# A lightweight convolution with a gated feed-forward on one core: the last values of the first pair put ahead of a multiply, and a new order of work for all later pairs

## The chip, the core and the metric

The kernel runs on one core of a Trainium2 chip. The core has TensorE (PE in the profile; its weight loads are listed apart as PEld), VectorE (DVE), ScalarE (ACT), GpSimd (POOL) and SyncE (SP), which issues most DMAs. The metric is the device time of a run in microseconds, the median of several runs. Lower is better.

## The reference

The input x has 8 sequences of 4096 tokens with 192 features, in float32. First comes a causal convolution over 7 tokens, whose taps are shared by each of 8 groups of 24 features (the kernel takes softmax of the taps once), then an RMS norm and a gated feed-forward:

```
w = softmax(weight, axis=-1)                      # 8 heads x 7 taps
y[b,s,h,g] = sum_k w[h,k] * x[b, s-6+k, h, g]     # zeros ahead of the sequence
xn  = y / sqrt(mean(y*y) + 1e-6) * rms_g          # over the 192 features
g   = xn @ w_gate                                 # 192 x 1536
val = xn @ w_val                                  # 192 x 1536
out = (silu(g) * val) @ w_out                     # 1536 x 192
```

The matrices arrive as 8-byte floats and are converted to 4-byte floats by the kernel itself (convert, L279): a few bit operations on VectorE, three activations on ScalarE, and for w_out an addition (L310) and a multiplication (L311) on GpSimd.

## The kernel before, in words

The 32768 tokens are worked on as 32 pairs, each of two blocks of 512 tokens (g = 0 and 1). Partitions 0 to 63 and 64 to 127 of TensorE's rows work at the same time on two halves: half 0 computes gates, half 1 values. Each half has four of the eight PSUM banks; `pick` and `free` decide which bank is handed out, in the order of the program.

**The first pair (pair 0)** is computed in the plain way by `plain` (L1001 products, L1011 silus on ScalarE, L1018 values = product times silu on VectorE), while the weights are still being converted. The string START says in which order parts are issued: p a product, s a silu, v a value, w a sum of weights, i/o/O conversions, c the convolution of pair 1, n one of five parts of the norm of pair 1 (square, reduce, factor, spread, scale; the last, `scale`, is the multiply of the outputs y by their factors, L499 on GpSimd), and t the placing of the normed pair 1 in DRAM (`place`, L623: eight DMAs, four of them for this pair alone on ScalarE's queue). LATER is a list of such letters with a due time each; it is merged with the output products of pair 0 (`outer`, L1034), with the taps of the convolution of pair 2 (`part_tap`, L429: the first tap on ScalarE, L437, six on VectorE, L445, summed up in a PSUM bank, the last one written to y), with its norm and with eleven sums of X (`x_sum`, L670), all by due time. `outer` has 12 row blocks per product, four products per output group; its values leave the banks by L1049 (ScalarE) and L1053 (VectorE).

**Pairs 1 to 31** use a scheme with fewer products. The class `Pair` runs 4 `Unit`s, which share chains of matrix products (`CHAINS`, L718): a product (v, i) adds the product of weight sum WAT[i] and X sum XOP[i] into bank v of the unit. Between the products the content of a bank is copied. Letters of the actions, each with the unit and half behind it (S42.1.0 is snapshot 42, half 1, unit 0):

- S: a snapshot of a bank into a tile; F: a fork, a copy of a bank into a new bank from which another chain goes on (`FORK`, with a sign)
- D: adds snapshot 00 to bank 5; C: bank 5 plus snapshot 40
- R: bank v plus or minus a snapshot (`RESULT`), a final gate (half 0) or value (half 1), which gives the bank free
- G: silu of a gate; M: value times gate
- S1 to S4 with one number: sums of h for the output (`Pair.sum`, L917); X: sums of X; cv: a tap (`part_tap`) of the pair after next; C1, s7, c2, C21, C22, T11 to T22: steps of the output; Dst0, Dst1: stores; DfetA, DfetB, Dplace, Dload: other DMAs; sq, red, pow, bc, mul: the five parts of the norm

A pair has 120 products (60 chain places x 2 halves, L757) and then nine output forms (`OUTS`, L889). The whole order is written out by hand in the string ORDER: p2 means two products of TensorE, A, V, G and D ahead of a name mean ScalarE, VectorE, GpSimd and a DMA; a name with a minus belongs to the pair before. Each engine works through its own instructions in that order.

Lines that the change and the prediction touch: ORDER, CHAINS, `Unit.do` (L763 to L804: S and F at L708/L712, D L773, C L777, R L781, G L794, M L801), START, LATER and the list `xat` of the X sums at the end.

Of the kernel before, what the change touches and what calls it, by code (L numbers as in the profile page):

```python
# [13 lines left out]
ALU = mybir.AluOpType  # L14
# [5 lines left out]
def kernel(  # L20
# [10 lines left out]
    nc = tc.nc  # L31
# [56 lines left out]

    SPAN = 1509
    ORDER = (  # L90
        "p2 VT11- p2 AS40.1.0 AS40.0.0 p2 Vbc- AF0.0.0 GX9- AF0.1.0 Dst0- p2 VC.1.0 Dload- GX4- VC.0.0 p2",
        "AS41.0.0 VS41.1.0 p1 AS00.0.0 p1 Gmul- VT21- AS00.1.0 p2 VD5.0.0 AS42.0.0",
        "VS42.1.0 p2 VD5.1.0 AS51.0.0 p2 Dst1- VR1.0.0 AS51.1.0 p2 VR1.1.0 AF2.0.0",
        "p2 AF2.1.0 VR0.0.0 Dplace- AG1.0.0 p1 VR0.1.0 p1 AF3.0.0 AF3.1.0 p2 VR2.0.0 AG0.0.0",
        "p1 VR2.1.0 p1 AS44.0.0 GM0.1.0 AS44.1.0 p2 VR3.0.0 AG2.0.0 GM1.1.0 p1 VR3.1.0 p1",
        "AS40.0.1 VR5.0.0 AS40.1.1 p2 AG4.0.0 VR5.1.0 AG5.0.0 p1 VM4.1.0 p1 AF0.0.1 VF0.1.1",
        "p2 AS41.0.1 VM5.1.0 AS41.1.1 p2 GM2.1.0 VC.0.1 AG3.0.0 p1 VC.1.1 p1 AS00.0.1 GM3.1.0",
        "AS00.1.1 p2 AS42.0.1 VS42.1.1 p2 GS3.0 VD5.0.1 p1 VD5.1.1 AS51.0.1 p1 GS3.1 VR1.0.1",
        "AS51.1.1 p2 VR1.1.1 AF2.0.1 p1 GS1.0 p1 AF2.1.1 VR0.0.1 AG1.0.1 p1 VR0.1.1 p1",
        "AF3.0.1 GM1.1.1 AF3.1.1 p2 VR2.0.1 p1 VR2.1.1 GS2.0 p1 AS44.0.1 AS44.1.1 p2 VR3.0.1",  # L100
        "AG0.0.1 p1 VR3.1.1 GM0.1.1 p1 AS40.0.2 VR5.0.1 AS40.1.2 p2 AG4.0.1 VR5.1.1 AG2.0.1",
        "p1 VM4.1.1 p1 AF0.1.2 GM2.1.1 VF0.0.2 p2 AS41.0.2 VS41.1.2 AG3.0.1 p2 VC.0.2 AG5.0.1",
        "GM3.1.1 p1 VC.1.2 p1 AS00.1.2 VS00.0.2 p1 GM5.1.1 p1 AS42.0.2 AS42.1.2 p2 VD5.0.2",
        "GS3.2 p1 VD5.1.2 AS51.0.2 p1 VR1.0.2 AS51.1.2 GS1.1 p2 VR1.1.2 AF2.0.2 p2 AF2.1.2",
        "VR0.0.2 GS1.2 AG1.0.2 p1 VR0.1.2 p1 AF3.0.2 GS2.1 AF3.1.2 p2 VR2.0.2 AG0.0.2 p1",
        "VR2.1.2 p1 AS44.0.2 GM0.1.2 AS44.1.2 p2 VR3.0.2 GM1.1.2 p1 VR5.1.2 p1 AS40.0.3",
        "VR5.0.2 AS40.1.3 p2 GS2.2 AG4.0.2 VR3.1.2 AG3.0.2 p1 VM4.1.2 p1 AG5.0.2 VF0.0.3 p2",
        "AF0.1.3 GM5.1.2 VS41.1.3 AS41.0.3 p2 AG2.0.2 VC.0.3 p1 VC.1.3 p1 AS00.0.3 VM2.1.2",
        "AS00.1.3 p2 AS42.0.3 GM3.1.2 AS42.1.3 p2 VD5.0.3 GS3.3 p1 VD5.1.3 AS51.0.3 p1",
        "VR1.0.3 AS51.1.3 p2 GS4.2 VR1.1.3 AF2.0.3 p2 AF2.1.3 VR0.0.3 GS1.3 p1 VR0.1.3 p1",  # L110
        "AF3.0.3 VF3.1.3 p2 GS3.4 AS44.1.3 VS44.0.3 AG1.0.3 p2 VR5.1.3 AG0.0.3 GM1.1.3 p1",
        "VR5.0.3 p1 VR3.0.3 AG5.0.3 p1 GS2.3 VR3.1.3 AG4.0.3 p2 Acv0_2 VM4.1.3 p2 Acv0_0",
        "GS4.3 VR2.0.3 DfetA p1 Acv0_1 p1 Vcv1_0 p1 AG3.0.3 p1 GM5.1.3 Vcv1_2 p3 VM3.1.3 p1",
        "Ac1 p1 GS3.5 Vcv2_0 p2 Vcv2_2 p2 GS1.4 Vcv1_1 p3 VM0.1.3 p2 GS1.5 Vcv2_1 p2 As7",
        "Vcv3_0 DfetB p1 AG2.0.3 p1 Vcv3_1 GS2.5 p2 Vcv3_2 p2 GS2.4 Vcv4_0 p2 VR2.1.3 p2",
        "GS4.0 Vcv4_2 p2 Vcv5_0 p2 GS4.4 p4 VX0 Ac2 p2 GS4.1 Vcv5_2 p2 Vcv4_1 p1 GX1 p1",
        "Vcv5_1 p2 Vcv6_0 p1 GM2.1.3 p1 Vcv6_2 p3 GX7 p3 GX3 p2 VC22 p2 Vcv6_1 p2 VT22 Asq p2",
        "VX2 p2 GS4.5 VC21 p1 Vred p2 GX6 p5 VX5 p2 VX8 p2 VX10 p1 Gpow VT12 p2",
    )

    cst = ctx.enter_context(tc.tile_pool(name="cst", bufs=1))
# [115 lines left out]
    def load_out(i):  # L237
# [28 lines left out]
        out=taps[:], in0=w_sb[:], in1=stat[:].to_broadcast([P, H, K]), op=ALU.subtract  # L266
# [7 lines left out]
        out=taps[:], in0=taps[:], in1=ssum[:].to_broadcast([P, H, K]), op=ALU.mult  # L274
# [419 lines left out]
    def put(at, do):  # L694
        heapq.heappush(line, (at, next(tick), do))
# [5 lines left out]
    def plus(s):  # L701
        return ALU.add if s > 0 else ALU.subtract
# [3 lines left out]
    def copy(eng, dst, src, s=1):  # L706
        if eng == "A":
            nc.scalar.activation(out=dst, in_=src, func=AF.Copy, scale=float(s))  # L708
        elif s < 0:
            nc.vector.tensor_scalar(out=dst, in0=src, scalar1=-1.0, scalar2=None, op0=ALU.mult)  # L710
        else:
            nc.vector.tensor_copy(out=dst, in_=src)  # L712
# [5 lines left out]
    CHAINS = [  # L718
        [(u, 4, 11)] + [(u - 1, 4, 0)] * (u > 0) + [(u, *c) for c in CHAIN] for u in range(NU)
    ]  # L720
    CHAINS[0][2:4] = CHAINS[0][3:1:-1]
    CHAINS[0][5:7] = CHAINS[0][6:4:-1]
    CHAINS[-1][-3:] = [(NU - 1, 4, 12), (NU - 1, 2, 1), (NU - 1, 3, 14), (NU - 1, 4, 0)]
    FORK = {0: (1, 1), 2: (4, 1), 3: (5, -1)}
    RESULT = {1: ("42", -1), 0: ("41", -1), 2: ("51", -1), 5: ("44", -1), 3: ("c", 1)}

    class Unit:
        def __init__(self, u):
            self.u = u
            self.ht = None  # L730
            self.bk, self.tl = {}, {}

        def new(self, v, h, product=False):
# [29 lines left out]
        def do(self, eng, act, h):  # L763
            tl, kind, v = self.tl, act[0], int(act[1:2] or 0)
            if kind == "S":
                t = tl[act[1:], h] = tiles.pop(0)
                copy(eng, t[:], self.old(v, h))
            elif kind == "F":
                src, s = FORK[v]
                copy(eng, self.new(v, h), self.old(src, h), s)  # L770
            elif kind == "D":
                b, t = self.old(5, h), tl.pop(("00", h))
                nc.vector.tensor_tensor(out=b, in0=b, in1=t[:], op=ALU.add)  # L773
                tiles.append(t)
            elif kind == "C":
                t = tl["c", h] = tl.pop(("40", h))
                nc.vector.tensor_tensor(out=t[:], in0=self.old(5, h), in1=t[:], op=ALU.add)  # L777
            elif kind == "R":
                k, s = RESULT[v]
                t = tl.pop((k, h))  # L780
                nc.vector.tensor_tensor(  # L781
                    out=self.hv(v) if h else t[:], in0=self.old(v, h), in1=t[:], op=plus(s)
                )
                self.leave(v, h)
                if h:
                    tiles.append(t)
                else:
                    tl["g", v] = t
            elif kind == "G":
                if v in RESULT:  # L790
                    t = src = tl["g", v]
                else:
                    t, src = tiles.pop(0), self.old(v, 0)
                nc.scalar.activation(out=t[:], in_=src[:], func=AF.Silu)  # L794
                if v not in RESULT:
                    self.leave(v, 0)
                tl["g", v] = t
            else:
                t = tl.pop(("g", v))
                src = self.hv(v) if v in RESULT else self.old(v, 1)  # L800
                engine[eng].tensor_tensor(out=self.hv(v), in0=src, in1=t[:], op=ALU.mult)  # L801
                if v not in RESULT:
                    self.leave(v, 1)
                tiles.append(t)  # L804
# [311 lines left out]
    def done(it):  # L1116
# [8 lines left out]

    START = (
        "XxxxxxXDdDdDTDdadTbTaTfbTakTakTakTkbkKkKkKkbkbfpoffpfsicpsvivOpsipisvicpsvpvwsicwpvs"
        "iwpvscwpsiwvpisvicpsvovpwispvswcipvwspsiwOvpsiwvipsvvpswopsvcpsvOnovoOpsonvOpsnoOvnopsoOn"
    )
    LATER = (  # L1130
        (55, "O"), (60, "t"), (163, "s"), (170, "O"), (200, "v"), (294, "v"),
        (463, "w"), (564, "w"), (664, "w"), (764, "w"), (864, "w"), (964, "w"), (1064, "w"),
        (1164, "w"), (1264, "w"),
    )
# [9 lines left out]
    p, sl, v = plain(hts)  # L1144
# [37 lines left out]
    for j in range(len(SIDE)):  # L1182
        put(c + 240 + 700 * (j // 2), functools.partial(part_tap, 2, 0, j))
        for k in range(1, K):
            at = c + 250 + 100 * k + 50 * j if j < 2 else c + 960 + 80 * k
# [3 lines left out]
    later(place(2), c + 2450)  # L1189
    xat = [c + i for i in (1660, 1730, 2060, 2130, 2200, 2270, 2290)]  # L1190
    xat += [c + i for i in (2360, 2370, 2380, 2390)]
    for i, at in enumerate(xat):
        put(at, functools.partial(x_sum, i))
    later(out_sums(), *[base + 2600 + 60 * i for i in range(4 * NM)])
    emit(float("inf"))
# [48 lines left out]
```

## Time and profile before

| | |
|---|---|
| median of 3 runs | 2607.96 us (2606.99 to 2608.02) |
| profiled execution, own time | 2610.66 us |
| its span | 2608.7 us |
| TensorE busy | 2575.5 us (99%), 23794 instructions |
| VectorE busy | 2272.6 us (87%), 3617 |
| ScalarE busy | 1618.6 us (62%), 2967 |
| GpSimd busy | 2081.1 us (80%), 1693 |
| TensorE clock granted, mean | 0.997 |

The span runs from the first to the last event of one profiled execution on the core; the execution's own time is 2 us longer than it, and 2.7 us longer than the median of the runs. Busy time says how long an engine had an instruction in work; where an engine is not the one that the others wait for, its idle time costs nothing. The granted clock is the share of full speed that the throttle of TensorE allowed. A time in the timeline counts from the start of the span.

### The profile page before, as it was taken

The numbers are of one execution on the slowest core, as the hardware profiler recorded it, in microseconds if no ns is written. First come the engines' busy times: TensorE is split into PE (matmuls) and PEld (weight loads), VectorE is DVE, ScalarE is ACT, GpSimd is POOL, SyncE is SP. The second block draws the span as 40 slices with busy tenths as digits, with TensorE's granted clock in tenths as the row PEclk, the third lists the DMA queues.
The fourth block names the chain that finished last, engine by engine and source line by source line (L and its number), as shares of the span: only waits on it lengthen the run. The fifth ranks groups of instructions, "written<-read, shape, count | busy, mean of one in ns | idle before, by whom it ended". The sixth has DMA issues, their size and how long they took to land.

```text
span 2608.7 us, 60700 instructions
## 1 busy us (share of the span) xinstructions
PE 2575.5 (99%) x23794; PEld 1869.1 (72%) x23794; DVE 2272.6 (87%) x3617; ACT 1618.6 (62%) x2967; POOL 2081.1 (80%) x1693
## 2 busy tenths in 40 slices
PE   6999999999999999999999999999999999999999
PEld 3677777777777766777777777777777777777776
DVE  8988888988888988898888889888888888888875
ACT  5375556765556765557655567655577555676554
POOL 3878788877888777888788887778887888887776
PEclk9999999999999999999999999999999999999999
DMA  6313321323312223213233122232132332232210
GB/s 144 56 39 57 63 47 42 63 39 63 63 35 54 51 51 63 50 39 63 39 63 63 37 52 51 51 63 52 38 61 40 62 63 42 47 60 41 50 38 13
DMA packets 512603, 137.36 MB, mean 53 GB/s; under 512 B 484284, under 2 KB 486844, under 8 KB 512189
## 3 DMA queue, kind: packets, MB, share of 16 engines
q1 hardware_dynamic: 509068, 132.80, 26.7%
q8 instruction: 186, 3.05, 0.5%
q10 hardware_dynamic: 3248, 0.69, 0.1%
q14 instruction: 101, 0.83, 0.1%
HBM read 83.87 MB, written 49.55 MB: 51 GB/s over the span
## 4 chain that ended last, share of the span: by engine, by line
PE 97%; DVE 2%; DMA 0%; ACT 0%; issue 0%; DVEq 0%; SPq 0%; ACTq 0%
PE ps L757 62%; PE ps L889 33%; PE ps L1041 1%; PE ps L1001 1%; DVE xc L304 0%; DMA x<-in_x_dram 0%; DVE ht L1018 0%; DVE y L406 0%; DVE y L421 0%; DVE y L394 0%; PE ps L595 0%; DVE wf L319 0%; ACT xb L615 0%; DVE xc L314 0%; DVE xc L287 0%
## 5 line engine op out<-in xcount | busy, mean ns | idle before, releaser
L757 PE MATMUL ps<-xc,wf 64*128 64x512 f32 x4960 | 1250.0, 592 | 0.0
L757 PEld LDWEIGHTS ps<-xc,wf 64*128 64x128 f32 x4960 | 755.4, 186 | 308.8 <-issue 66.2
L757 PE MATMUL ps<-xb,wf 64*128 64x512 f32 x2480 | 710.4, 589 | 0.0
L801 POOL TENSOR_TENSOR ht<-ht,tile 128x512 f32<-128x512 f32 x298 | 378.8, 1280 | 277.1 <-ACT tile L794 275.1
L708 ACT ACTIVATE tile<-ps 128x512 f32<-128x512 f32 (+1 forms) x677 | 391.0, 593 | 319.5 <-PE ps L757 190.1
L708 ACT ACTIVATE tls<-ps 128x512 f32<-128x512 f32 (+1 forms) x656 | 376.1, 589 | 314.9 <-PE ps L889 192.7
L757 PEld LDWEIGHTS ps<-xb,wf 64*128 64x128 f32 x2480 | 391.9, 187 | 143.6 <-issue 30.7
L708 ACT ACTIVATE ps<-ps 128x512 f32<-128x512 f32 (+1 forms) x651 | 366.9, 578 | 54.0 <-PE ps L889 39.0
L917 POOL TENSOR_TENSOR early<-ht 128x512 f32<-128x512 f32 x279 | 379.4, 1365 | 4.9
L889 PE MATMUL ps<-ht,wo_sb 128*32 128x128 f32 (+2 forms) x5208 | 318.6, 380 | 0.0
L445 DVE SCALAR_TENSOR_TENSOR ps<-xh,tp,ps 128x512 f32<-128x512 f32 x450 | 312.0, 745 | 1.2
L801 POOL TENSOR_TENSOR ht<-ht,tls 128x512 f32<-128x512 f32 x198 | 251.6, 1277 | 76.2 <-ACT tls L794 74.6
L781 DVE TENSOR_TENSOR tile<-ps,tile 128x512 f32<-128x512 f32 x366 | 250.1, 687 | 62.8 <-PE ps L757 56.1
L889 PEld LDWEIGHTS ps<-ht,wo_sb 128*32 128x32 f32 x5208 | 234.2, 110 | 81.5 <-POOL ht L801 23.5
L889 PE MATMUL ps<-ht,x 128*32 128x128 f32 (+2 forms) x4464 | 250.7, 379 | 0.0
L917 POOL TENSOR_TENSOR ht<-ht 128x512 f32<-128x512 f32 x186 | 248.2, 1351 | 0.0
L794 ACT ACTIVATE tile<-tile 128x512 f32<-128x512 f32 x366 | 228.2, 629 | 12.5 <-DVE tile L781 12.5
L889 PEld LDWEIGHTS ps<-ht,x 128*32 128x32 f32 x4464 | 184.6, 110 | 61.1
L781 DVE TENSOR_TENSOR ht<-ps,tile 128x512 f32<-128x512 f32 x322 | 219.1, 681 | 0.1
L781 DVE TENSOR_TENSOR ht<-ps,tls 128x512 f32<-128x512 f32 x298 | 202.7, 680 | 0.0
L889 PE MATMUL ps<-early,x 128*32 128x256 f32 (+2 forms) x3348 | 196.0, 379 | 0.0
L781 DVE TENSOR_TENSOR tls<-ps,tls 128x512 f32<-128x512 f32 x254 | 173.9, 685 | 25.1 <-PE ps L757 23.6
(129 smaller groups left out, 3176.9 us busy)
## 6 DMA issues: line engine op xcount, KB each, us to landing
xb<-xd SPq DMA_DIRECT2D x124, 384.0 KB
xd<-yn SPq DMA_DIRECT2D x244, 96.0 KB
xh<-in_x_dram SPq DMA_DIRECT2D x192, 105.0 KB
out_dram<-o_sb SPq DMA_DIRECT2D x122, 96.0 KB
out_dram<-o_sb SPq DMA_DIRECT2D x62, 128.0 KB
xh<-in_x_dram SPq DMA_DIRECT2D x56, 98.4 KB
out_dram<-o_sb SPq DMA_DIRECT2D x122, 32.0 KB
ht<-in_moe_w_gate_dram SPq DMA_DIRECT2D x12, 192.0 KB
```

Source lines behind the costliest of these rows:

```text
L445: nc.vector.scalar_tensor_tensor(out=dst, in0=xk, scalar=w, in1=at, op0=ALU.mult, op1=ALU.add)
L708: nc.scalar.activation(out=dst, in_=src, func=AF.Copy, scale=float(s))
L757: nc.tensor.matmul(out=self.new(v, h, True) if first else self.old(v, h), lhsT=wf[self.u][HALF[h], WAT[i], :], rhs=x_op(XOP[i])[HALF[h]], ...
L781: nc.vector.tensor_tensor(out=self.hv(v) if h else t[:], in0=self.old(v, h), in1=t[:], op=plus(s))
L794: nc.scalar.activation(out=t[:], in_=src[:], func=AF.Silu)
L801: engine[eng].tensor_tensor(out=self.hv(v), in0=src, in1=t[:], op=ALU.mult)
L889: nc.tensor.matmul(out=self.bank(b)[i * Q : (i + 1) * Q, at : at + n], lhsT=left, rhs=cols, start=fresh, stop=True, skip_group_check=True, ...
L917: engine[eng].tensor_tensor(out=dst, in0=a, in1=b, op=op)
L1001: nc.tensor.matmul(out=bank(h, bks[h])[:], lhsT=wf[u][HALF[h], k * NF + f, :], rhs=xb[HALF[h], g, k, :], start=(k == 0), stop=(k == KP - 1 ...
L1041: nc.tensor.matmul(out=bank(h, bks[h])[:, w : w + D], lhsT=hts[f // NF][HALF[h], g, f % NF, j * P : (j + 1) * P], rhs=wo_sb[HALF[h], f, :] ...
```

## The change

The change has four parts.

1. In unit 0 of every pair the products (4,7) and (0,3) change places, so that (4,7) stands directly ahead of (5,2) and (2,1).
2. The upper half of bank 2 in unit 0 is no longer a copy of bank 4 (AF2.1.0 is gone). A new action N on VectorE takes snapshot 51 of the upper half away from bank 4; product (2,1) then finds no bank for (2, upper half), takes one with start=True and so begins afresh; and R2 adds the snapshot instead of subtracting it. The value is the same. Units 1 to 3 keep the fork.
3. ORDER is new. Per pair ScalarE has 87 actions instead of 92, VectorE 108 instead of 106, GpSimd 51 instead of 48. Snapshots S00.0.0, S00.0.1, S41.0.1, S41.0.3, S42.0.3, S44.1.3 and forks F3.0.1, F3.0.2, F3.0.3 go to VectorE; S00.0.2, S41.1.3, S44.0.3, F0.0.3 and F3.1.3 go to ScalarE; the multiplies M0.1.3, M2.1.2, M3.1.3 and M5.1.0 go to GpSimd, M2.1.3 to VectorE; X0, X2 and X8 go to GpSimd, X1, X3 and X6 to VectorE. The place DMAs, the stores, the norm's parts and the taps have new places: T21 and Dst1 now stand at their own pair's end, Dst0 behind DfetB of the next pair.
4. In the first pair START loses its last n (the multiply L499), and LATER issues the last silu and the last two values first, with the last conversions of w_out between and after them, and then the multiply and the placing. The first eleven X sums have a new order too.

The diff, without most of ORDER:

```diff
     SPAN = 1509
     ORDER = (
-        "p2 VT11- p2 AS40.1.0 AS40.0.0 p2 Vbc- AF0.0.0 GX9- AF0.1.0 Dst0- p2 VC.1.0 Dload- GX4- VC.0.0 p2",
-        "AS41.0.0 VS41.1.0 p1 AS00.0.0 p1 Gmul- VT21- AS00.1.0 p2 VD5.0.0 AS42.0.0",
-        "VS42.1.0 p2 VD5.1.0 AS51.0.0 p2 Dst1- VR1.0.0 AS51.1.0 p2 VR1.1.0 AF2.0.0",
-        "p2 AF2.1.0 VR0.0.0 Dplace- AG1.0.0 p1 VR0.1.0 p1 AF3.0.0 AF3.1.0 p2 VR2.0.0 AG0.0.0",
...
-        "Vcv3_0 DfetB p1 AG2.0.3 p1 Vcv3_1 GS2.5 p2 Vcv3_2 p2 GS2.4 Vcv4_0 p2 VR2.1.3 p2",
...
+        "p2 GX4- VT11- p2 AS40.0.0 GX9- AS40.1.0 p2 AF0.1.0 AF0.0.0 p2 VC.0.0 Dload- p2",
+        "VC.1.0 AS41.0.0 VS41.1.0 p2 AS00.1.0 VS00.0.0 p2 Vbc- VD5.0.0 Gmul- p2 VD5.1.0",
+        "AS42.0.0 VS42.1.0 AS51.1.0 p2 AS51.0.0 VR1.0.0 p2 VR1.1.0 VR0.0.0 p2 AF2.0.0 VN.1.0",
+        "AG0.0.0 p2 VR0.1.0 AF3.0.0 Dplace- AF3.1.0 p2 GM0.1.0 VR2.0.0 p2 VR2.1.0 AS44.1.0",
...
+        "Vcv5_1 p1 GM0.1.3 p1 Vcv3_0 p2 Vcv6_1 p1 GS2.5 p1 Vcv4_0 p2 Vcv4_2 GS4.0 p2 Vcv5_0",
...
     CHAINS[0][2:4] = CHAINS[0][3:1:-1]
     CHAINS[0][5:7] = CHAINS[0][6:4:-1]
+    CHAINS[0][8:10] = CHAINS[0][9:7:-1]
@@
             self.ht = None
+            self.ahead = False
@@
+            elif kind == "N":
+                t = tl["51", h]
+                nc.vector.tensor_tensor(
+                    out=t[:], in0=self.old(4, h), in1=t[:], op=ALU.subtract
+                )
+                self.ahead = True
@@
                 k, s = RESULT[v]
+                if v == 2 and h and self.ahead:
+                    s = 1
@@
-        "iwpvscwpsiwvpisvicpsvovpwispvswcipvwspsiwOvpsiwvipsvvpswopsvcpsvOnovoOpsonvOpsnoOvnopsoOn"
+        "iwpvscwpsiwvpisvicpsvovpwispvswcipvwspsiwOvpsiwvipsvvpswopsvcpsvOnovoOpsonvOpsnoOvnopsoO"
     )
     LATER = (
-        (55, "O"), (60, "t"), (163, "s"), (170, "O"), (200, "v"), (294, "v"),
+        (30, "s"), (35, "v"), (40, "O"), (45, "v"), (50, "O"), (55, "n"), (60, "t"),
         (463, "w"), (564, "w"), (664, "w"), (764, "w"), (864, "w"), (964, "w"), (1064, "w"),
@@
-    for i, at in enumerate(xat):
+    for i, at in zip((0, 1, 7, 2, 3, 5, 6, 10, 8, 9, 4), xat):
         put(at, functools.partial(x_sum, i))
```

## The prediction, made before the changed kernel had run

> **What bounds the kernel now.** I read the head and the chain of work that ended last first: they say which engine sets the end.
>
> ```profile
> span 2608.7 us, 60700 instructions
> ...
> PE 97%; DVE 2%; DMA 0%; ACT 0%; issue 0%; DVEq 0%; SPq 0%; ACTq 0%
> PE ps L757 62%; PE ps L889 33%; PE ps L1041 1%; PE ps L1001 1%; DVE xc L304 0%; DMA x<-in_x_dram 0%; DVE ht L1018 0%; DVE y L406 0%; DVE y L421 0%; DVE y L394 0%; PE ps L595 0%; DVE wf L319 0%; ACT xb L615 0%; DVE xc L314 0%; DVE xc L287 0%
> ```
>
> TensorE carries it. What VectorE, ScalarE or GpSimd gain counts only where TensorE waits for them. The same chain piece by piece around the first pair (columns: start, us, what):
>
> ```profile
> 106.62 3.14 DVE xc L304
> 109.76 0.61 DVE ht L1018
> 110.37 0.04 issue
> 110.41 30.03 PE ps L1041 x325
> ...
> 220.25 51.98 PE ps L757 x240
> 272.23 27.44 PE ps L889 x337
> ```
>
> So a pair is 51.98 + 27.44 = 79.42 us, and this repeats 31 times; the one hole after start-up that the chain leaves TensorE for is at 107 to 110 us. Third, the timeline of the engines at that hole (VectorE, ScalarE, GpSimd, TensorE):
>
> ```profile
> 105.52 1.17 DVE L294 TENSOR_SCALAR xc<-tls 128x384 uint32<-128x384 uint32 x1
> 106.62 3.14 DVE L304 SCALAR_TENSOR_TENSOR xc<-tls,xc 128x384 uint32<-128x384 uint32 x1
> 109.68 0.68 DVE L1018 TENSOR_TENSOR ht<-ps,tile 128x512 f32<-128x512 f32 x1
> ...
> 113.58 6.67 DVE L445 SCALAR_TENSOR_TENSOR ps<-xh,tp,ps 128x512 f32<-128x512 f32 x10
> 120.16 1.40 DVE L445 SCALAR_TENSOR_TENSOR y<-xh,tp,ps 128x512 f32<-128x512 f32 x2
> ```
> ```profile
> 109.41 2.89 ACTq L635 DMA_DIRECT2D xd<-yn  x4
> 112.35 0.60 ACT L1011 ACTIVATE tile<-ps 128x512 f32<-128x512 f32 x1 [4.65 <-POOL wf L350]
> 112.84 1.90 ACT L437 ACTIVATE ps<-xh,tp 128x512 f32<-128x512 f32 x3
> ```
> ```profile
> 106.44 2.94 POOL L499 TENSOR_TENSOR yn<-y,s 128x1536 f32<-128x1536 f32 x1
> 109.30 1.32 POOL L310 TENSOR_TENSOR xc<-xc,tls 128x384 f32<-128x384 f32 x1
> 110.70 0.99 POOL L311 TENSOR_TENSOR wo_sb<-xc 128x384 f32<-128x384 f32 x1
> ```
> ```profile
> 110.41 16.87 PE L1041 MATMUL ps<-wo_sb,ht 64*128 64x192 f32 x168 [2.90 <-DVE ht L1018]
> ```
>
> TensorE stands 2.90 us for the last but one value, queued on VectorE behind a conversion step (L304) that takes 3.14 us beside GpSimd's multiply. The windows by stage put the mean granted clock of 111 to 141 us at 0.91 and of 96 to 111 at 0.95: 30 x 0.09 + 15 x 0.05 = 3.45 us lost, or 6.9 us at half speed, beginning just after the hole. Some 3.0 us of that falls on running products.
>
> Fourth, TensorE's weight loads in a pair that starts at 379.02:
>
> ```profile
> 386.01 0.43 PEld L757 LDWEIGHTS ps<-xc,wf 64*128 64x128 f32 x4 [0.65 <-ACT tile L708]
> ```
>
> This is product (4,7) of unit 0, whose bank is snapshot (S42) shortly before. Its passes come at 7.53 us after the pair's start where the 0.429 us rhythm would give 7.44: 0.09 us lost per pair. I find two more such losses in it, 0.04 (a load waiting for C of the lower half) and 0.10 (at the pair's start), which the change leaves.
>
> **What the Trainium skill says.** "TensorE: Matmul & The Clock Gate", Part 1 ("What's actually happening"): the clock falls to half after an idle window of about 3.4 us, windows run freely. The trace agrees roughly: a hole of 3 us, then about 6.9 us at half. The same page, "Terms" and the table ahead of it: ScalarE, VectorE and GpSimd are strict first-in first-out, TensorE draws weight loads forward. The trace agrees: silu 24 (L1011) sits out four DMA issues. "GPSIMD Engine Reference", section 1: GpSimd shares SBUF interfaces with VectorE instructions of two SBUF inputs; here L304 takes 3.14 us beside L499 and 1.09 to 1.17 otherwise. "PSUM — Partial Sum Buffer", "The four PSUM rules": a first matmul overwrites the bank, so bank 2's upper half needs no copy into it; each copy takes 0.58 us here (L708 ps<-ps).
>
> **The first pair.** The normalization's last part ("n", L499) and four place DMAs ("t") leave their old position; the last two values and silu 24 move ahead. VectorE's queue becomes L294, value 23, value 24, L304; GpSimd's L310, L311, L499; ScalarE's silu 24, L298, L299, L302, DMAs, first taps.
> Gain: value 23 runs at 106.6 to 107.3 and TensorE does not stand: -2.9, and the half clock at 109.6 is not called up: -3.0.
> Cost: L304 runs after the values, 107.96 to 109.1 (1.17 without L499 beside it). The last L310 starts behind L302 (ends 107.7), L311 behind L304, 109.1 to 110.1. L499 takes 110.1 to 113.0 instead of 106.44 to 109.38, +3.6. The place DMAs on ScalarE's queue (2.89 us) end at 115.9; behind them the first tap L437 starts at 115.95 instead of 112.84, +3.1, and VectorE's taps (L445) start at 116.6 instead of 113.58. The first y of the three tap banks ends at 120.86 + 3.0 = 123.87.
> Who waits: the first row of the second output group, on bank 1, lower half, 65 rows after the one that stood, needs that bank back from the tap's y on VectorE. A pair of rows takes 0.3255 us at full clock. Before, TensorE came there at 110.41 + 32 x 0.3255 + 3.0 = 123.8, when the bank had been free since 120.9. Now it comes at 107.4 + 10.4 = 117.9 and stands until 123.87: 6.0 us. It goes on at the same moment as before (+0.1). The hole is twice as long, so half clock again; on the grid of 6.83 us on which the recorded clock changes (109.6, 116.4, 123.3, 130.1) it lasts to 130.1, costing (130.1 - 123.9)/2 = +3.1; if only one window of 3.4 us, +1.4. Sum of the first pair: +3.2 (or +1.5), because the gain of 5.9 is spent at the next wait. The landing of xb and the X sums, some 3 us later (to about 141), still precede pair 1's first product (143.5). The permuted X sums cost the same eleven instructions.
>
> **Each later pair.** (4,7) and (0,3) change places. S42 lies one index (0.86 us) further ahead: the 0.09 goes. But the fork of bank 4 to bank 2's lower half (F2.0.0, ScalarE, 0.58) now starts only after (4,7): pass ends 8.30, bank drained and fork started 8.92, ended 9.50, load of (2,1) at 9.55, pass at 10.09 against 10.01 nominal: +0.07. Net -0.02 per pair, 31 x 0.02 = -0.6. That the upper half starts afresh removes one 0.58 us copy from ScalarE, and adds N (VectorE, 0.69) in a gap before R2: off the path, ended at 9.88 against a load at 10.4.
> New order: ScalarE loses 5 operations (62% busy), VectorE gains 2 (87%), GpSimd gains 3 (80%). I followed each bank's and tile's release against the load that needs it: the tightest come 0.08 to 0.2 us ahead of it, so I cost them at nothing; if one is late by d, it costs 31 d. The stores and place DMAs moved along SP's queue meet it idle. GpSimd: from M1.1.3 (50.70, which waits for its data in both) to sum S2.5 it has ten instructions instead of eight, at 1.24 us pitch 2.5 us more, less 2 x 0.45 that two sums lose beside VectorE's multiplies, which move away: S2.5 ends at 63.3 instead of 61.8. Form 6 loads it at 65.0: hidden, with 1.7 us left.
>
> **Sum.** 3.2 - 0.6 = +2.6 on the profiled execution's 2610.66, that is 2613.3; it lies 2.7 over the median 2607.96, so the median becomes about 2610.6. A measurement of this kernel tells 0.2% (5.2 us), so: within it.
>
> **Rivals.**
> A, TensorE does not stand at bank 1, 0.10: then -2.9 - 3.0 - 0.6 = -6.5, 2601.5. For it: those two losses are real rows. Against: the taps' bank is released by a queue that L499 and the DMAs hold back.
> B, slower, 0.30: GpSimd's added multiplies make S2.5 late. It decides from 1.7 us of further delay per pair, since TensorE then waits in each of 31 pairs; 0.3 us beyond gives +9.3 + 2.6, 2619.9; from 0.09 beyond, it shows. For it: GpSimd has 3 us less slack there, and its durations go from 1.28 to 1.77 beside VectorE instructions of two SBUF inputs, whose places the new order shifts. Against: four such collisions at 0.45 are needed.
> C, the wait at unit 0 goes wholly, the fork being in time, with less lag between the halves, 0.14: -0.10 to -0.2 per pair, -3 to -6 + 3.2, 2605 to 2608.
> D, the change does not do what it says at (2,1), since the lower half still waits for its copy: contained in my forecast.
>
> **How the numbers follow.** Forecast 0.44, with its own range 2607 to 2613.5 (half clock 1.4 or 3.1, pairs -0.05 to +0.03); A 0.10, B 0.30, C 0.14; 0.02 for the rest. A, and a small part of C, are faster: 0.13. B is slower nearly always, 0.29, with some of the forecast's upper tail: 0.31. The remainder, 0.56, is within 0.2%. The range 2603 to 2619.5 leaves out most of A and the long end of B.
>
> **What would show it.** A wait of L1051 for VectorE's y (L445) of some 6 us from 118 to 124, no hole at 107, and the clock low from about 123 and not from 109.6. A pair of 51.96 + 27.44, the late load at (2,1) and none at (4,7). L889's (now L899) loads of sums must not wait on GpSimd; a stage of outputs longer than 27.44 would prove B, a wait of tens of loads by 0.1 in the products another late release that I costed at nothing.

## The result, and the profile after

| | before | changed |
|---|---|---|
| median | 2607.91 us (22 runs) | 2612.51 us (22 runs) |
| lowest to highest | 2606.45 to 2610.98 | 2610.37 to 2613.81 |
| profiled execution, own time | 2610.66 | 2610.37 |
| its span | 2608.7 | 2608.6 |

The ratio over all runs is 1.0014 with the interval 1.0008 to 1.0021, some 3.7 us longer; the medians part by 4.6 us. Both are below the 5.2 us (0.2%) that the prediction takes as what a measurement of this kernel tells. The medians part by more because the runs of the kernel before fall in two groups, 14 of 2606.4 to 2608.0 us and 8 of 2609.2 to 2611.0, and its median lies in the shorter one. The two profiled executions are alike in length, and that misleads: the one of the changed kernel is the shortest of its 22 runs, and the one of the kernel before belongs to the longer group. The experiments show what parts the groups.

The chain of the changed kernel (start, us, what) has a new hole in the first pair and pairs that are a little shorter:

```profile
105.08 1.27 DVE ht L1028 x2
...
122.77 0.75 DVE y L445
123.57 18.39 PE ps L1051 x195
...
380.10 51.92 PE ps L759 x240
432.02 27.44 PE ps L899 x337
```

A pair takes 51.92 + 27.44 = 79.36 us instead of 79.42. The timelines of TensorE, ScalarE, VectorE and GpSimd in the first pair answer to the four shown of the kernel before. This execution reached that place some 1.5 us earlier, as its first input DMA was shorter (8.75 against 9.54 us in the chain) and its first block of L595 too (3.94 against 4.65), with 3.4 us of start-up at half clock instead of 6.8; the change has no part in that.

```profile
101.75 15.05 PE L1051 MATMUL ps<-wo_sb,ht 64*128 64x192 f32 x177
123.57 7.67 PE L1051 MATMUL ps<-wo_sb,ht 64*128 64x192 f32 x66 [6.77 <-DVE y L445]
```
```profile
111.67 3.59 ACTq L635 DMA_DIRECT2D xd<-yn  x4
115.46 1.91 ACT L437 ACTIVATE ps<-xh,tp 128x512 f32<-128x512 f32 x3 [9.30 <-DMA xd<-yn]
```
```profile
105.08 1.27 DVE L1028 TENSOR_TENSOR ht<-ps,tile 128x512 f32<-128x512 f32 x2
106.27 1.39 DVE L304 SCALAR_TENSOR_TENSOR xc<-tls,xc 128x384 uint32<-128x384 uint32 x1
116.18 6.68 DVE L445 SCALAR_TENSOR_TENSOR ps<-xh,tp,ps 128x512 f32<-128x512 f32 x10 [8.52 <-ACT ps L437]
122.77 1.40 DVE L445 SCALAR_TENSOR_TENSOR y<-xh,tp,ps 128x512 f32<-128x512 f32 x2
```
```profile
107.81 1.01 POOL L311 TENSOR_TENSOR wo_sb<-xc 128x384 f32<-128x384 f32 x1 [0.56 <-DVE xc L304]
108.76 2.87 POOL L499 TENSOR_TENSOR yn<-y,s 128x1536 f32<-128x1536 f32 x1
```

Read from the bottom up: the multiply now stands behind the last conversion, the place DMAs behind the multiply, the first taps behind the DMAs, the y that frees bank 1 behind the taps, and TensorE stands 6.77 us for it. The two values at the top are done at 106.35, so the old hole of 2.90 us is gone. The windows by stage show the clock that the hole calls (after the length, the busy time of TensorE, its weight loads, VectorE, ScalarE and GpSimd; the last three figures are granted clock, DMA share, GB/s):

```profile
119.90:123.30 3.40, 0.00 (x0) 0.00 (x0) 3.40 (x6) 0.00 (x0) 3.09 (x8) 0.65 0.93 220
123.30:126.70 3.40, 3.13 (x20) 3.13 (x22) 3.29 (x6) 0.00 (x0) 3.01 (x8) 0.50 1.08 217
126.70:130.10 3.40, 3.40 (x40) 3.40 (x37) 2.48 (x4) 1.28 (x1) 1.66 (x4) 0.85 0.08 15
```

It falls while TensorE stands (at 120.9), and of its 6.8 us at half speed about 4.2 fall on running products: 2.1 us lost.

In a later pair, the late weight load is one at (2,1), waiting for the fork on ScalarE, and no longer the one at (4,7):

```profile
389.55 0.30 PEld L759 LDWEIGHTS ps<-xc,wf 64*128 64x128 f32 x4 [0.64 <-ACT ps L708]
```

The start times of the products in the trace give, per pair, an excess over the 0.429 us rhythm of 0.078 us there. The two excesses of before at C (0.041) and at (4,7) (0.093) are gone; the one at the pair's start (0.104) stays. 0.078 - 0.041 - 0.093 = -0.056, which is the difference of the pairs.

### The profile page after: what moved, and what is told of

Read it like the earlier page. It is cut to its first block, busy times and chain, and to the rows that moved or that the text cites. A ratio compares the mean times of both kernels' runs of the same rounds, so it can differ in the third digit from the quotient of the medians.

```text
span 2608.6 us, 60634 instructions
## 1 busy us (share of the span) xinstructions
PE 2572.9 (99%) x23794; PEld 1756.9 (67%) x23794; DVE 2309.3 (89%) x3679; ACT 1545.0 (59%) x2812; POOL 2189.0 (84%) x1786
## 4 chain that ended last, share of the span: by engine, by line
PE 96%; DVE 2%; issue 0%; DMA 0%; ACT 0%; POOL 0%; ACTq 0%; DVEq 0%; SPq 0%; POOLq 0%
PE ps L759 62%; PE ps L899 33%; PE ps L1011 1%; PE ps L1051 1%; DMA x<-in_x_dram 0%; DVE ht L1028 0%; DVE xc L304 0%; DVE y L406 0%; DVE y L421 0%; DVE ps L445 0%; DVE y L394 0%; DVE wf L319 0%; ACT xb L615 0%; PE ps L595 0%; ACTq L635 0%
## 5 line engine op out<-in xcount | busy, mean ns | idle before, releaser
L759 PE MATMUL ps<-xc,wf 64*128 64x512 f32 x4960 | 1216.6, 591 | 0.0
L759 PEld LDWEIGHTS ps<-xc,wf 64*128 64x128 f32 x4960 | 680.5, 186 | 376.8 <-issue 181.3
L759 PE MATMUL ps<-xb,wf 64*128 64x512 f32 x2480 | 682.3, 591 | 0.0
L708 ACT ACTIVATE tile<-ps 128x512 f32<-128x512 f32 x678 | 391.2, 593 | 389.7 <-PE ps L759 296.1
L708 ACT ACTIVATE tls<-ps 128x512 f32<-128x512 f32 (+1 forms) x562 | 323.4, 589 | 437.9 <-PE ps L759 221.4
L811 POOL TENSOR_TENSOR ht<-ht,tile 128x512 f32<-128x512 f32 x329 | 419.0, 1275 | 144.2 <-ACT tile L804 65.6
L759 PEld LDWEIGHTS ps<-xb,wf 64*128 64x128 f32 x2480 | 354.0, 187 | 183.0 <-issue 96.3
L811 POOL TENSOR_TENSOR ht<-ht,tls 128x512 f32<-128x512 f32 x260 | 330.6, 1274 | 86.2 <-ACT tls L804 40.4
L708 ACT ACTIVATE ps<-ps 128x512 f32<-128x512 f32 (+1 forms) x589 | 336.1, 581 | 88.0 <-PE ps L899 32.6
L927 POOL TENSOR_TENSOR early<-ht 128x512 f32<-128x512 f32 x279 | 354.9, 1277 | 5.1 <-POOL ht L811 0.3
L899 PEld LDWEIGHTS ps<-ht,wo_sb 128*32 128x32 f32 x5208 | 233.9, 110 | 81.7 <-POOL ht L811 23.5
```

Source lines behind the costliest of these rows:

```text
L759: nc.tensor.matmul(out=self.new(v, h, True) if first else self.old(v, h), lhsT=wf[self.u][HALF[h], WAT[i], :], rhs=x_op(XOP[i])[HALF[h]], ...
L899: nc.tensor.matmul(out=self.bank(b)[i * Q : (i + 1) * Q, at : at + n], lhsT=left, rhs=cols, start=fresh, stop=True, skip_group_check=True, ...
L927: engine[eng].tensor_tensor(out=dst, in0=a, in1=b, op=op)
```

## The experiments

Two theories stood against each other. Mine: the first pair spends at bank 1 what it gains at the old hole, and the pairs gain a little. The rival: the new order of the later pairs costs the time.

**The first pair alone.** The kernel before with START, LATER and the order of the first X sums of the changed one:

```diff
-        ... "OvnopsoOn"
+        ... "OvnopsoO"
-        (55, "O"), (60, "t"), (163, "s"), (170, "O"), (200, "v"), (294, "v"),
+        (30, "s"), (35, "v"), (40, "O"), (45, "v"), (50, "O"), (55, "n"), (60, "t"),
...
-    for i, at in enumerate(xat):
+    for i, at in zip((0, 1, 7, 2, 3, 5, 6, 10, 8, 9, 4), xat):
```

> The kernel before with the first pair's part of the change alone (START, LATER, order of the first X sums); all later pairs as before. Theory (the gain at the old hole is spent at bank 1, and the longer hole always calls the half clock): a wait of TensorE for VectorE's y of 6 to 7 us at about 117 to 124 and no hole at 107; later pairs 79.42 us with losses at (4,7) and C as before; median 2612.5 to 2615, that is +5 to +7 over the kernel before where that ran without a fall of the clock, +3 where it ran with one. Rival (the slowness comes from the new order of the later pairs): within 1 us of the kernel before.

Measured: median 2614.39 us, ratio to before 1.0022 (1.0014 to 1.0030). The waits of TensorE (total, times, longest) and the chain of a later pair:

```profile
PE ps L1041 <- DVE y L445: 6.8, 1, 6.8
```
```profile
222.59 51.98 PE ps L757 x240
```

The loss is here: the 6.8 us wait is that of the changed kernel, and the pairs are those of before. In this trace four of the 30 steps from pair to pair are 0.2 to 0.4 us longer, which makes all pairs together 1.2 us longer than before; why is open.

**The new order alone.** The changed kernel with START and LATER of before (the same lines the other way round); the order of the first X sums stays that of the changed one.

> The changed kernel with START and LATER as before: the new order, the chain swap and the fresh upper half alone. Theory: pairs of 79.36 instead of 79.42 us, 31 x -0.056 = -1.7, median about 2606; the hole at 107 to 110 as before. Rival (new order costs time in some pairs): above the kernel before by 2 to 4 us.

Measured: median 2607.36 us, ratio 0.9992 (0.9984 to 1.0000), pairs as in the changed kernel:

```profile
216.73 51.92 PE ps L759 x240
```

The new order saves: in the traces, from the first product of pair 1 to the last output product, 2461.4 us against 2463.0, so 1.6. By the ratios the first pair alone costs some 5.7 us and the order alone saves some 2.1; the sum, +3.6, is about the +3.7 of the whole change. Each interval is 2 us wide to either side, so the sum is a rough one.

**The two groups of runs of the kernel before.** It was profiled three times more, unchanged.

> The kernel before, unchanged, looked at once more. Its 22 runs fall in two groups, near 2607.5 and near 2610.8. Theory: the hole of 3 us at 107 calls the half clock only in the runs near 2610.8 (the windows of the clock run freely), so a run near 2607.5 shows full clock through 110 to 141 us and the output products of the first pair 3 us shorter (27 instead of 30). Rival (the groups come from the start-up, as its first input DMA): the clock is low after the hole in both.

> The kernel before once more, to find an execution of its other group. Theory: with about 2607 us the output products of pair 0 after the hole take 27 us at full clock; with about 2610.5 they take 30 us and the clock is low from 109.6. Rival: no such tie between the time and the clock.

> As the look before it: a time near 2607 goes with 27 us of output products at full clock, one near 2610.5 with 30 us. Rival: no such tie.

These executions took 2610.6, 2606.76 and 2606.97 us. Timeline of TensorE in the first of them and then in the second:

```profile
110.57 29.88 PE L1041 MATMUL ps<-wo_sb,ht 64*128 64x192 f32 x325 [2.90 <-DVE ht L1018]
```
```profile
109.48 27.08 PE L1041 MATMUL ps<-wo_sb,ht 64*128 64x192 f32 x325 [2.93 <-DVE ht L1018]
```

The windows of the same two:

```profile
111.00:141.00 30.00, 30.00 (x331) 29.96 (x331) 23.95 (x37) 5.69 (x9) 24.07 (x42) 0.91 0.64 121
```
```profile
111.00:141.00 30.00, 30.00 (x334) 28.24 (x330) 25.68 (x41) 8.34 (x14) 24.09 (x43) 1.00 0.63 116
```

The same hole of 2.9 us, and once the clock falls behind it (325 products in 29.88 us), once it does not (27.08). The third of them ran at full clock with 27.08, and so did the new order alone, whose START and LATER are those of before; the execution profiled first had the fall (30.03). So the fall costs 2.8 to 2.9 us. That is most of the 3.6 to 3.9 us by which the longer executions differ from the shorter. The rest lies ahead of the hole, which begins 0.8 to 1.1 us later in the two longer ones: there the start-up had 6.8 us at half clock, in the two shorter ones 3.4. So the rival, the start-up, has a share. On three occasions 8 of 22, 16 of 25 and 17 of 33 runs of the kernel before took more than 2608.5 us, about half in all; that each of these had the fall is inferred from the four that were profiled.

**The fork kept.** The changed kernel with the copy on ScalarE in place of N:

```diff
-        "... p2 AF2.0.0 VN.1.0",
+        "... p2 AF2.0.0 AF2.1.0",
```

> The changed kernel with the fork of bank 4 kept for the upper half of bank 2 in unit 0 (AF2.1.0 on ScalarE in place of N on VectorE). Prediction's claim (that part is off the path): pairs of 79.36 us as in the changed kernel, the late load at (2,1) of 0.078 unchanged. Rival (starting afresh is what made room for the swap): a second late load in the upper half, pairs longer by 0.05 us or more.

Measured: 2622.32 us in a single run, pairs of 52.26 + 27.44 = 79.70. The chain, then the weight loads:

```profile
383.11 52.26 PE ps L759 x239
```
```profile
392.55 0.29 PEld L759 LDWEIGHTS ps<-xc,wf 64*128 64x128 f32 x2 [0.63 <-ACT ps L708]
393.04 0.29 PEld L759 LDWEIGHTS ps<-xc,wf 64*128 64x128 f32 x3 [0.20 <-ACT ps L708]
```

The upper half of (2,1) now waits for the second of two copies one behind the other, 0.46 us late, and the halves' lag runs on into later loads: +0.34 us per pair, which repeats in nearly every pair of the trace. In this order of work the fresh bank is what makes the swap affordable.

**Both halves fresh.** The changed kernel with N for the lower half as well:

```diff
-        "... p2 AF2.0.0 VN.1.0",
+        "... p2 VN.0.0 VN.1.0",
-                if v == 2 and h and self.ahead:
+                if v == 2 and self.ahead:
```

> The changed kernel in which bank 2 of unit 0 begins afresh in both halves: the fork AF2.0.0 is replaced by N on VectorE for the lower half too. Theory (the one late load left in unit 0 waits for that fork): the 0.078 us late pass at (2,1) goes, pairs of about 79.28, 31 x -0.078 = -2.4 against the changed kernel, median about 2610. Rival (the load is late for another reason, as the start of a bank): pairs stay at 79.36, median about 2612.5.

Measured: median 2621.78 us; pairs of 79.71 us, 0.35 more. The chain and the loads:

```profile
380.86 52.27 PE ps L759 x240
```
```profile
392.52 0.18 PEld L759 LDWEIGHTS ps<-xb,wf 64*128 64x128 f32 x1 [0.28 <-ACT ps L708]
```

The late pass at (2,1) did go, as the theory has it, and the time still rose: the next R actions on VectorE run 0.6 us later behind the added N, the fork F3 of the upper half waits for one of them, and (3,14) is late; late passes of 0.05 to 0.26 us stand at the next three places of the chain, and two of 0.10 to 0.15 in unit 2, which I did not follow up. My expectation of 2610 was wrong.

**The C of the lower half last again.** The changed kernel with the order of before for these two actions:

```diff
-        "... p2 VC.0.0 Dload- p2",  "VC.1.0 AS41.0.0 ...",
+        "... p2 VC.1.0 Dload- p2",  "VC.0.0 AS41.0.0 ...",
```

> The changed kernel with the two C actions of unit 0 in the order of before (upper half first, then lower half, on VectorE). The pairs gained 0.056 us, the prediction had 0.02, as it left the 0.041 of the late load after C untouched. Theory (the new order puts the lower half's C first, and that took the 0.041 away): pairs of 79.40 us, a late pass of 0.04 at about 4.4 us after the pair's start in both halves. Rival (the loss went for another reason): 79.36.

Measured: 2613.3 us in a single run; the pair is back at 51.96 + 27.44 = 79.40, with the late pass of 0.042 at 4.32 us in both halves.

```profile
382.37 51.96 PE ps L759 x240
```

**The queue that holds bank 1.** Three kernels move single things in the first pair of the changed one. The first puts the two first taps ahead of the place DMAs on ScalarE's queue (all other engines keep their order):

```diff
-        put(c + 240 + 700 * (j // 2), functools.partial(part_tap, 2, 0, j))
+        put(c - 60 + 1000 * (j // 2), functools.partial(part_tap, 2, 0, j))
-            at = c + 250 + 100 * k + 50 * j if j < 2 else c + 960 + 80 * k
+            at = c - 50 + 8 * k + 4 * j if j < 2 else c + 960 + 80 * k
-        ... (55, "n"), (60, "t"),
+        ... (55, "n"), (200, "t"),
```

> The changed kernel with one move: on ScalarE's queue the two first taps (L437) of the convolution of pair 2 stand ahead of the four place DMAs instead of behind them. Theory (TensorE waits 6.8 us at bank 1 because those taps wait out L499 and the DMAs): the first y ends near 115 instead of 123.5, no wait at L1051, full clock through 111 to 141, output products of pair 0 end about 10 us earlier (6.8 wait + 3.3 half clock); the X sums (from about 127.5, when xb has landed) may then hold the next pair by up to 2 us; median 2602.5 to 2605. Rival (bank 1 is late for another reason, as the y buffer that L499 reads): the wait stays at 3 us or more and the median above 2608.

Measured: median 2607.58 us. The wait at bank 1 is gone wholly, so the release by the taps is the cause of it. But 2607.6 is above what I expected; the chain and TensorE's timeline of the profiled execution say what came instead:

```profile
121.13 10.30 DMA xb<-xd
```
```profile
137.16 2.04 PE L759 MATMUL ps<-xc,wf 64*128 64x512 f32 x6 [3.01 <-DVE xc L670]
140.20 1.22 PE L759 MATMUL ps<-xc,wf 64*128 64x512 f32 x1 [1.00 <-DVE o_sb L1063]
```

TensorE is at pair 1 at 134.2, and the X sums (L670) are late, since they follow the landing of xb, which follows L499 and the place DMAs. It waits 3.0 + 1.0 us, the clock falls again, at 139, and the first of the later pairs takes 84.05 us. This execution, of 2610.23 us, is the longest of the kernel's 13 runs (the shortest took 2605.40), so it shows the dearest case, and the others may have lost less. The landing of xb takes 10.3 us in the chain, 8.6 in the kernel with both moves below. In both of them the load of the next input starts at about 121.7 instead of 128.87, beside xb; that this is what makes xb slow is not tested.

The second puts only the multiply back ahead of the last two conversions, on GpSimd's queue:

```diff
-        ... "OvnopsoO"
+        ... "OvnopsoOn"
-        (30, "s"), (35, "v"), (40, "O"), (45, "v"), (50, "O"), (55, "n"), (60, "t"),
+        (30, "s"), (35, "v"), (45, "v"), (47, "O"), (50, "O"), (60, "t"),
```

> The changed kernel with one move: on GpSimd's queue the multiply L499 stands ahead of the last two conversions (L310, L311), as in the kernel before; the values stay ahead on VectorE. Theory: place DMAs and taps run 3 to 4 us earlier, TensorE's wait at bank 1 shrinks from 6.8 to about 3 us; the half clock then comes in some runs only: median 2605.5 (without) to 2609 (with). Rival (the place of the multiply does not matter): 2612.5 as the changed kernel.

Measured: median 2606.02 us, ratio 0.9993 (0.9984 to 1.0001); the profiled execution, of 2606.04 us, has the wait of 3 us, and a clock of 0.94 over 111 to 141 us (3.4 us at half speed behind the wait, so 1.7 lost):

```profile
PE ps L1051 <- DVE y L445: 3.0, 1, 3.0
```

The third has both moves.

> The changed kernel with both moves: the multiply L499 ahead of the last conversions, and the two first taps ahead of the place DMAs. Theory: no wait at bank 1, no half clock, and xb lands 3 to 4 us earlier than with the taps alone, so nothing holds the next pair: median about 2602, at least as fast as with the taps alone. Rival: L304 takes 3.1 us beside L499 and holds the taps back until a wait of 1 us or more at bank 1 returns: 2604 or more.

Measured: median 2602.74 us, ratio to before 0.9978 (0.9970 to 0.9987), faster than both kernels. VectorE, and the windows:

```profile
107.03 2.00 DVE L304 SCALAR_TENSOR_TENSOR xc<-tls,xc 128x384 uint32<-128x384 uint32 x1
108.95 6.67 DVE L445 SCALAR_TENSOR_TENSOR ps<-xh,tp,ps 128x512 f32<-128x512 f32 x10
115.53 1.39 DVE L445 SCALAR_TENSOR_TENSOR y<-xh,tp,ps 128x512 f32<-128x512 f32 x2
```
```profile
111.00:141.00 30.00, 29.89 (x309) 27.18 (x307) 26.22 (x42) 7.72 (x13) 26.10 (x46) 1.00 0.71 126
```

y is there at 116.3, some 1.2 us before TensorE wants bank 1, and there is no hole and no fall of the clock. L304 takes 2.00 us, partly beside L499, against 1.39 alone: too little to matter. From the first output product of pair 0 to the first product of pair 1 it takes 32.0 us; the changed kernel takes 41.0, the kernel before 35.0 without the fall of the clock and 37.9 with it.

## Why the prediction was right, and where not

It named 2610.6, no change that can be measured; measured were 2612.51, and a change of 0.14% by all runs (0.18% by the medians). That the figure came within 2 us is in part luck: a saving of 3.0 us that half of the runs don't have, and a gain in the pairs that was 1.0 us too small, partly made up for each other.

**First pair: right.** The gain at the value (2.9) came. The wait at bank 1 came, at the row and for the y named: 6.8 us instead of 6.0, for the most part because the four place DMAs took 3.59 us instead of 2.89, the duration of before that I had used. The fall of the clock behind it cost 2.1 where I had 3.1, on a grid of 6.83 us: the records have stretches of 3.4, 6.8 and 10.2 us at half clock, and here one begins 2.7 us before TensorE goes on. In the other traces with this wait the fall cost 2.0 to 2.8. In sum +3.1 us against a run of before with the fall (41.0 - 37.9); I had +3.2, so near because the two errors, +0.8 and -1.0, nearly cancel. I also had L304 at 1.17 us away from L499, as one such instruction took; others of its shape took 0.54 to 1.37 before, and this one 1.39. The chain through L311, L499, the DMAs and the taps is shown by the two single moves, each of which shortens the wait (to 3.0, to none).

**The step that failed: the clock gain booked on the median.** I took the sum on the profiled execution and carried it to the median with its constant distance of 2.7 us. That distance was for the most part the fall of the clock: the profiled execution had it, and the three runs shown (2606.99 to 2608.02) lie in the shorter group, which by the traces runs without it. Against an execution without it the first pair costs 41.0 - 35.0 = +6.0, and the sum is +6.0 - 1.6 = +4.4, where the medians part by 4.6. "The half clock is not called up, -3.0" holds for the longer group alone, 8 of the 22 runs here and about half of all.

**Later pairs: the new loss right, one gain missed.** The loss at (2,1) is 0.078 us where I worked out 0.07, the gain at (4,7) 0.093 as read. That the loss after C (0.041) stays was wrong: the new order does the lower half's C first, which the run with the old order of C shows. So -0.056 per pair instead of -0.02; 31 times that is -1.7 instead of -0.6 (the traces have -1.6 in all).

**"Off the path": wrong for the fork.** I costed the removal of the upper half's copy at nothing. With the copy kept the swap costs 0.34 us per pair, 10.5 us over 31 pairs. It is nothing only against the kernel before, where (4,7) stood one index earlier and no product at (2,1) was late.

**Rivals.** A (TensorE does not stand at bank 1) and C (the wait at unit 0 goes wholly) fell. B (GpSimd's sums come late) fell: the output stage stays at 27.44 us in each kernel with the new order, and the loads' wait for GpSimd's L811 is 23.5 us in both traces. That the other late releases cost nothing stands, as far as the pairs show no further late pass that sets their length.

**What the skill says** of the clock, "TensorE: Matmul & The Clock Gate", Part 1 ("What's actually happening"), that it falls after an idle window of about 3.4 us and that the windows run freely, agrees in the second part: the clock changes here on steps of 3.41 us that lie differently in each execution, and a hole of 2.9 us calls the half clock in some executions and not in others. A hole of 6.8 us did so in each of the five traces with it. In the first part the runs differ, and they decide: holes of 2.88 to 3.01 us, shorter than such a window, called the half clock in four of seven traces.

## What to carry to other kernels

When a wait is taken away, follow TensorE forward to the next thing it needs and ask whether that was moved back by the same edit; here the next bank was held by a chain over four queues, and the gain came back as a longer hole. Before a sum is carried from a profiled execution to a median, look at the clock in it: an execution with a hole near the length of the clock's steps (here 3 of 3.4 us) can belong to one of two groups. And a copy that is hidden now can be what another edit needs out of the way: cost such pairs of edits together.

## What the hardware showed beyond what was expected

The same hole of 2.9 us costs 2.8 to 2.9 us more or nothing: of five profiled executions with that hole, two had the fall. What decides is where the hole lies. In each trace all changes of the recorded clock are whole multiples of 3.413 us apart. Cut at these steps, the holes of about 3 us divide so:

| trace | hole, us | its parts in two neighbouring steps | clock then |
|---|---|---|---|
| before | 2.89 | 2.10 + 0.79 | half for 6.83 us |
| before, 2610.6 us | 2.90 | 1.80 + 1.10 | half for 6.83 us |
| multiply first | 2.95 | 0.71 + 2.25 | half for 3.41 us |
| taps before the place DMAs | 3.01 | 1.34 + 1.68 | half for 6.83 us |
| new order alone | 2.90 | 1.62 + 1.28 | full |
| before, 2606.76 us | 2.93 | 1.38 + 1.55 | full |
| before, 2606.97 us | 2.88 | 1.37 + 1.52 | full |

With 1.68 us or more of idle time in one step, about half of it, the next step is at half clock; with 1.62 or less (1.66 in one step of a longer hole) it is not. This is read off seven traces after the fact, the ends of products being modelled, and it holds for this part of the kernel alone: during the start-up, steps with 1.7 to 1.95 us of idle time were followed by full clock.

The four place DMAs on ScalarE's queue took 2.88 to 2.89 us in the traces with the first pair of before and 3.45 to 3.65 in those with a changed one. L304 took 3.14 us almost wholly beside the multiply L499, 2.00 partly beside it and 1.39 away from it.
